# A sigmoid attention and token-mixing kernel: a new order of steps, loads and banks, merged stores, and the output weights rearranged by four transfers

## The chip, the cores and the metric

The kernel runs on one core of one Trainium2 chip. The metric is the device time of one execution in microseconds (us), the median over several runs. Lower is better.

## The reference

Attention with a sigmoid in place of the softmax, and on its output a layer that mixes tokens with weights made from the tokens themselves:

```python
# q, k, v: [8 batches, 12 heads, 448 tokens, 64]
scores = q @ k.T / sqrt(64) - log(448)
attn = 1 / (1 + exp(-scores))
x = (attn @ v)                      # heads side by side: [8, 448, 768]
wq, wk = x @ w_q, x @ w_k           # [8, 448, 64] each
W_tok = einsum('bsd,btd->bst', wq, wk) / sqrt(64)
mixed = einsum('bst,btd->bsd', W_tok, x)
out = maximum(mixed, 0) @ w_out     # [8, 448, 768], float32
```

## The kernel before

**Units of work.** Four heads of a batch make a quad; there are 24 quads (8 batches by 3). Tokens are numbered so that token = 7 p + i, with p on 64 partitions and i from 0 to 6, so each quad has 7 blocks of keys. One step `S` is one block: four score matmuls (L319) into two banks and one sigmoid of 128 x 896 elements on ScalarE, called ACT here (L324), into one of 16 `at` buffers. There are 168 such steps. A step `P` multiplies one block of `at` with the values (L341); after the seventh block of a quad the sum is copied out of the banks to `xt` (L348 in halves on two engines, L350 whole).

**What q, k and v go through.** The sync engine's queue (SP) loads each quad's q, k and v in float32 (L173, L179) into 8 buffers, GpSimd (POOL) or another engine casts them to bf16 (L192, L209, L215). Quads differ in how q and k are transposed. Kind `c` (14 quads): six copies of 32-partition pieces rearrange q and k on GpSimd (`arrange`, L161, L164, L167), then VectorE (DVE) transposes each whole (L276). Kind `r` (6 quads): VectorE transposes them in six pieces (L245, L269). Kinds `a` and `q`: TensorE (PE) transposes them (L237, L229), and VectorE copies the result.

**The mixing.** For each batch `tr_x` transposes `xt` to `xn` (L363, L379), `mlp_wqk` (L404, L416) makes wq and wk, `mlp_wkn` and `mlp_tmp` (L445, L460) and `mlp_mix` (L484, L498) follow, with the relu at L469 (ACT) or L471 (VectorE). The output product works on pairs of batches: `out_chunk` (L611) takes 128 tokens at a time for the first and the last pair, two token blocks of 64 at once, and stores them by `store` (L618 to L624), one transfer for each block; `out_pair` (L530) does the two pairs in the middle and `out_halves` (L570) a part of the last. `out_pair` and `out_halves` use a second copy of the output weights with its partition halves exchanged, made by step `C`, which moves `wout16` within the on-chip memory by SP (L864).

**The order.** Everything runs in an order written out by hand or by a planner: `PLAN` is a string with one letter for each step (`S`, `P`, `x` ...; a lower or an upper case often chooses the engine that copies a result out), `BANKS` says which of the eight PSUM banks each step takes, and `ORDER` is the order of the loads and casts; a dot there means a cast on VectorE, issued where `PLAN` has a `1`. Each engine executes its own instructions in that order and waits on semaphores. `pump_loads` issues a load as soon as the cast of the load eight before it has been issued; once `LATE` loads are out, only two more for each finished output chunk.

Of the kernel before, what the change touches and what calls it, by code (L numbers as in the profile page):

```python
# [17 lines left out]
def kernel(  # L18
# [12 lines left out]
    nc = tc.nc  # L31
    B, H, S, HD = q.shape
    D = H * HD
    DH = moe_w_q.shape[1]
    assert DH == HD == 64 and S == 448 and D == 768
    P = 128
    NI, NP = 7, 64
    NU = B
    NJ = H // 4
    NC = D // P  # L40
    NB = D // 2
    HALF = (slice(0, 64), slice(64, 128))
# [5 lines left out]
    def pool(name, bufs, **kw):  # L48
# [16 lines left out]
    banks16 = banks.rearrange("p b x -> p (b x)").bitcast(BF16).rearrange("p (b x) -> p b x", b=8)  # L65

    BANKS = (
# [11 lines left out]
    )  # L79
    BANKS = BANKS.split()[::-1]  # L80

# [25 lines left out]
    wout16 = singles.tile([P, 2 * NC, D], BF16, name="wout16")  # L107
# [17 lines left out]
    def xt(u, j):  # L125
        return xts[u % 2 * NJ + j]


    TW = (1, 2,)


    PLAN = (
        "FFSSSFFKSSF11aSSbFFrSFSFSSFSqSPPsPPSPzkPSPSPPPSxSrSsPPPPSPPS"
        "PSPPPPSSXWzSSwWWSWWXSNSSPPPrSsPPUSPPzSPSPSPCMPPPSPSqkSSMSXSM"
        "SCcPPPSPPxSPdPSOSwwrSSwwWWxSOSSOsOSNPPSPPzCPSPPSIISISIcPSPdP"
        "PSPS2SPPOOSxSUSPPSMPPPcSPPSdOwWwSSMWWWoSMPPSPPPP1SSPcdOQSxSO"
        "OSSNCSOOXcdSSOOSTSPPPSrPPCPSPPCPPSPPPSPSOwowSSSwsOzOxSwwWPSP"
        "MSPPPPRSScSdXXOXoSMSOoNSMPPSPcPPSPPSUdSOSMOSOMoPSPPcPPSPSdPw"
        "WXWSMSWWWXSSONOScTSOSOSOOdSPOSrOSPPPGPPSPPPSPPsPSPOSPOSOzSQS"
        "XPcPPSPPPSPOSOdSOSxOlLlSLlLPSPPPxPP2GSPOOScOmdOSOOSNO1SQSTPP"  # L140
        "PcS1PPSPOPSOSOQSMOSOSOdScOOSdOMSOmOP2PSPPxSPPP12SOSOSOSxOllL"
        "SllcSLPPPSPPPSPOOdSxSOOSOSOSONQSTPSPPPSPPPSPPPxPPmPPLxLlMlGL"
        "lOOyOoNIItIiIMimIiMOoOOOoOoOOOOOOOOOoOO"
    )
    KIND = ["a"] + [t for t in PLAN if t in "qacer"]

    ld = {}
    SRC = dict(q=q, k=k, v=v)
# [1 line left out]
    pq, arranged = {}, set()  # L150

    def arrange(n, eng):

        arranged.add(n)
        if KIND[n] in "er":
            return
        w = pq[n].rearrange("p e t i d y -> p e (t i d y)").bitcast(U32)
        z = p_one.tile([P, 2 * NI * 32], U32, tag="swap", name="swap")
        for g in range(2):
            lo, hi = slice(64 * g, 64 * g + 32), slice(64 * g + 32, 64 * g + 64)  # L160
            eng.tensor_copy(out=z[lo], in_=w[hi, 0])  # L161
        for g in range(2):
            lo, hi = slice(64 * g, 64 * g + 32), slice(64 * g + 32, 64 * g + 64)
            eng.tensor_copy(out=w[hi, 0], in_=w[lo, 1])  # L164
        for g in range(2):
            lo = slice(64 * g, 64 * g + 32)
            eng.tensor_copy(out=w[lo, 1], in_=z[lo])  # L167

    def load1(n, nm, eng):
        u, j = quads[n]  # L170
        if KIND[n] in "cer" and nm != "v":
            t = p_ld.tile([P, 2 * NI * HD], F32, tag="ld", name=nm + "32")
            eng.dma_start(  # L173
                out=t, in_=SRC[nm][u, 4 * j : 4 * j + 4].rearrange("h (p r) d -> (h p) (r d)", r=2 * NI),
            )
            ld[nm, n] = t
            return
        t = p_ld.tile([P, 2, NI * HD], F32, tag="ld", name=nm + "32")
        eng.dma_start(  # L179
            out=t,  # L180
            in_=SRC[nm][u, 4 * j : 4 * j + 4].rearrange(
                "(g h) (p i) d -> (h p) g (i d)", g=2, i=NI
            ),
        )
        ld[nm, n] = t

    def cast1(n, nm, e):
        if KIND[n] in "cer" and nm != "v":
            if n not in pq:
                pq[n] = p_c16.tile([P, 2, 2, NI, 32, 2], BF16, tag="qk16", name="qk16")  # L190
            f = pq[n]
            COPY[e](  # L192
                out=f[:, :, "qk".index(nm)].rearrange("p e i d y -> p e y i d"),
                in_=ld.pop((nm, n)).rearrange("p (y i e d) -> p e y i d", y=2, i=NI, e=2),
            )
            ld[nm + "16", n] = f
            if ("q16", n) in ld and ("k16", n) in ld:
                arrange(n, nc.gpsimd)
            return
        if nm == "v":  # L200
            t16 = p_v16.tile([P, 2, NI, HD], BF16, tag="v16", name="v16")
            if e == "d":
                u, j = quads[n]
                nc.gpsimd.dma_start(
                    out=t16.rearrange("p b i d -> p b (i d)"),
                    in_=v[u, 4 * j : 4 * j + 4].rearrange("(g h) (p i) d -> (h p) g (i d)", g=2, i=NI),
                )
            else:
                COPY[e](  # L209
                    out=t16.rearrange("p b i d -> p (b i d)"), in_=ld.pop((nm, n)).rearrange("p b x -> p (b x)"),  # L210
                )
            ld["v16", n] = t16
            return
        t16 = p_c16.tile([P, NI, 2, HD], BF16, tag=nm + "16", name=nm + "16")
        COPY[e](  # L215
            out=t16.rearrange("p i b d -> p b i d"),
            in_=ld.pop((nm, n)).rearrange("p b (i d) -> p b i d", i=NI),
        )
        ld[nm + "16", n] = t16
# [41 lines left out]
    def tr(n, nm, kind):  # L261
        t = "qk".index(nm)
        if kind == "s":
            return
        if kind == "r":
            qk[n] = p_qk.tile([P, 2, 2, NI, NP], BF16, tag="qk", name="qk")
            w = pq[n].rearrange("p e t i d y -> p e (t i d y)").bitcast(F32)
            for e in range(2):
                nc.vector.transpose(out=qk[n][:, e].rearrange("p t i n -> p (t i n)").bitcast(F32), in_=w[:, e])  # L269
            return  # L270
        if kind in "cdef":
            assert n in arranged
            w = pq[n].rearrange("p e t i d y -> p e (t i d y)").bitcast(F32)[:, t]
            if t == 0:
                qk[n] = p_qk.tile([P, 2, 2, NI, NP], BF16, tag="qk", name="qk")
            nc.vector.transpose(out=qk[n][:, t].rearrange("p t i n -> p (t i n)").bitcast(F32), in_=w)  # L276
            if kind in "ef":
                if t == 0:
                    moves.append((n, p_mv.tile([P, 2, 2 * S], BF16, tag="mv", name="mv")))
                nc.vector.transpose(out=moves[-1][1][:, t].bitcast(F32), in_=w)  # L280
            return
# [232 lines left out]
    def slot(half, b):  # L514

        return b // 2 + (0 if b % 2 == half else NC)

    def out_pair(act, split):

        if opened:  # L520
            w, blocks, part, fb, ps = opened.pop()
# [71 lines left out]
    def out_chunk(act, tail):  # L593
# [22 lines left out]
        last = w == NU // 2 - 1 and m == NI - 1  # L616

        def store(cols, eng=nc.scalar if tail else nc.sync):  # L618
            for y in range(2):
                b, i = divmod(2 * m + y, NI)  # L620
                (eng if y else nc.sync).dma_start(
                    out=out[2 * w + b].rearrange("(p i) d -> p i d", i=NI)[:, i, cols],
                    in_=o[HALF[y], cols],
                )  # L624
# [67 lines left out]
    for t in wqks:  # L692
# [1 line left out]


    ORDER = (
# [4 lines left out]
    )  # L701
    BY = {"s": [], "v": []}
    for x in ORDER.split():
# [7 lines left out]
    done = dict.fromkeys("SPqkKxWNUMOCgz", 0)  # L711
    used, loaded, cast = set(), set(), set()

    LATE = 44
    ring = [("q", 0), ("k", 0)]

    allowed = [2]
# [94 lines left out]
    used |= {("q", 0), ("k", 0)}  # L812
    pump()

    ALIKE = dict(a="q", c="q", e="q", r="q", b="k", d="k", f="k", s="k", j="k", h="k", X="x", y="x", Y="x", g="g", z="z", L="W", l="W", T="U", t="U", I="O", i="O", Q="O", G="M", R="P")
    done["q"] = done["k"] = 1
    quads_r = []

    for t in PLAN:
# [18 lines left out]
        elif kind in "qk":  # L838
# [4 lines left out]
            tr(c, kind, t)  # L843
            if t in "df":
                used.add(("q", c))
            if t not in "cers":
                used.add((kind, c))
                pump()
        elif t == "g":
# [10 lines left out]
        elif kind == "W":  # L860
            mlp_wqk(*divmod(c, NC), tail, t in "wl", t in "Ll")
        elif kind == "C":
            for y in range(2):
                nc.sync.dma_start(out=wout16[HALF[y], NC + c, :], in_=wout16[HALF[1 - y], c, :])  # L864
        elif kind == "N":
            mlp_wkn(c)
        elif kind == "U":
# [51 lines left out]
```

## Time and profile before

| what | value |
|---|---|
| median of 3 runs | 182.45 us (180.83 to 184.24) |
| span of the profiled execution (the page gives no other time for it) | 180.4 us |
| granted TensorE clock | 1.00 |
| busy: PE, DVE, ACT, POOL | 170.3, 143.7, 159.0, 122.9 us |
| sigmoids (L324) | 168, mean 951 ns each, 139.8 us in all |
| moved by DMA | 47.29 MB, 262 GB/s over the span |

The span runs from the first to the last instruction. Busy time is the union of an engine's instructions: two that overlap count once, so 168 sigmoids of 951 ns make 139.8 us. PE's matmuls are pipelined, and a PE that is busy all the time isn't at its peak for it. In lines by group, the columns are line, engine, operation, what is written and read with shapes and types, the number of instructions; then busy us and mean ns of one; then the idle time ahead of them, with what ended it.

### The profile page before, as it was taken

The page shows a single profiled execution, that of the slowest core. Times are in us where ns is not written, and L with a number is a line of the kernel's source. Part 1 is how long each engine was busy: PE and PEld are TensorE (multiplying, and loading weights), DVE is VectorE, ACT ScalarE, POOL GpSimd, SP SyncE. Part 2 cuts the span into 40 slices and gives each one's busy share as a digit, 9 for nine tenths or more (in the row PEclk, how much of TensorE's full clock was granted, in tenths as well). Part 3 has the DMA queues.
Part 4 walks back from the last instruction along what each step waited for, and adds up shares of the span by engine and source line. Part 5 has one row for each costly group of instructions (what it writes and reads, how often), then busy time and mean ns, then how long its engine had stood idle before and what let it go on. Part 6 is the DMA issues. An engine that isn't in the chain of part 4 may idle for free.

```text
span 180.4 us, 7849 instructions
## 1 busy us (share of the span) xinstructions
PE 170.3 (94%) x3412; PEld 114.1 (63%) x3412; DVE 143.7 (80%) x226; ACT 159.0 (88%) x208; POOL 122.9 (68%) x167
## 2 busy tenths in 40 slices
PE   7898899889999999999999999999999999999990
PEld 7444445444675555546667786677888888888660
DVE  3566899998988896989999999978789885868351
ACT  4599999999999999999999999998999989976310
POOL 1076899798999999999999999889978810010000
PEclk9999999999999999999999999999999999999999
DMA  5999999999999989699997999968596432505876
GB/s 169 353 394 346 325 385 376 283 304 366 339 305 358 349 266 299 226 318 349 279 318 277 257 307 329 372 215 272 137 336 166 131 88 48 137 4 123 207 196 174
DMA packets 24914, 47.29 MB, mean 262 GB/s; under 512 B 3888, under 2 KB 18480, under 8 KB 24880
## 3 DMA queue, kind: packets, MB, share of 16 engines
q1 hardware_dynamic: 23600, 44.64, 76.8%
q0 software_dynamic: 800, 1.18, 3.6%
q10 hardware_dynamic: 480, 0.98, 1.5%
q8 instruction: 26, 0.43, 0.9%
q14 instruction: 8, 0.07, 0.1%
HBM read 35.78 MB, written 11.01 MB: 259 GB/s over the span
## 4 chain that ended last, share of the span: by engine, by line
PE 61%; DMA 16%; ACT 7%; POOL 5%; DVE 4%; SPq 3%; issue 2%; POOLq 0%
PE banks L530 15%; PE banks L341 11%; PE banks L319 11%; PE banks L611 9%; DMA k<-in_k_dram 8%; ACT at L324 7%; DMA v<-in_v_dram 5%; DMA w<-in_moe_w_k_dram 4%; PE banks L570 3%; POOL qk L192 2%; PE banks L404 2%; PE banks L416 2%; PE banks L379 2%; PE banks L363 2%; PE banks L484 1%
## 5 line engine op out<-in xcount | busy, mean ns | idle before, releaser
L324 ACT ACTIVATE at<-banks 128x896 bf16<-128x896 f32 x168 | 139.8, 951 | 2.9 <-PE banks L319 2.4
L319 PE MATMUL banks<-qk 64*64 64x448 bf16 x672 | 62.0, 357 | 3.3 <-ACT at L324 2.0
L341 PE MATMUL banks<-at,v 64*64 64x448 bf16 x672 | 47.3, 351 | 0.8 <-ACT at L324 0.7
L319 PEld LDWEIGHTS <-qk 64*64 64x64 bf16 x672 | 25.7, 105 | 21.5 <-issue 13.3
L530 PE MATMUL banks<-wout,mx 64*64 64x384 bf16 x672 | 36.2, 323 | 0.0
L192 POOL CAST qk<-k 128x896 bf16<-128x896 f32 x19 | 22.7, 1196 | 10.1 <-DMA k<-in_k_dram 9.7
L341 PEld LDWEIGHTS <-v 64*64 64x64 bf16 x672 | 23.2, 106 | 8.4 <-issue 1.8
L350 DVE CAST xt<-banks 128x896 bf16<-128x896 f32 x22 | 23.8, 1084 | 2.5 <-PE banks L341 2.0
L530 PEld LDWEIGHTS <-mx 64*64 64x64 bf16 x672 | 22.6, 107 | 4.5 <-issue 0.2
L611 PE MATMUL banks<-wout,mx 128*128 128x384 bf16 (+1 forms) x138 | 24.4, 320 | 0.0
L192 POOL CAST qk<-q 128x896 bf16<-128x896 f32 x18 | 21.5, 1193 | 2.5 <-DVE qk L276 1.0
L471 DVE TENSOR_SCALAR mx<-banks 128x1024 bf16<-128x1024 f32 (+3 forms) x22 | 21.3, 970 | 1.9 <-PE banks L484 0.7
L209 POOL CAST v<-v 128x896 bf16<-128x896 f32 x22 | 20.6, 952 | 1.8 <-DMA v<-in_v_dram 1.3
L611 PEld LDWEIGHTS <-mx 128*128 128x128 bf16 x138 | 12.3, 98 | 9.8 <-issue 3.2
L167 POOL COPY qk<-swap 32x448 uint32<-32x448 uint32 x28 | 16.3, 584 | 1.6
L276 DVE STREAM_TRANSPOSE qk<-qk 128x448 f32<-128x448 f32 x28 | 17.0, 628 | 0.5 <-POOL qk L164 0.4
L161 POOL COPY swap<-qk 32x448 uint32<-32x448 uint32 x28 | 15.6, 556 | 2.5 <-DVE qk L192 0.8
L164 POOL COPY qk<-qk 32x448 uint32<-32x448 uint32 x28 | 15.6, 555 | 1.6
L245 DVE STREAM_TRANSPOSE qk<-qk 32x448 f32<-32x448 f32 x24 | 15.3, 636 | 0.6
L413 POOL COPY wq<-wqk 64x448 bf16<-64x448 bf16 x3 | 1.7, 556 | 15.8 <-DVE wqk L412 15.8
L644 DVE COPY o<-banks 128x384 f32<-128x384 f32 x12 | 6.6, 553 | 5.7 <-PE banks L611 5.3
L392 DVE COPY xn<-banks 128x1024 bf16<-128x1024 bf16 (+1 forms) x14 | 8.8, 625 | 2.8 <-PE banks L379 2.7
(89 smaller groups left out, 203.8 us busy)
## 6 DMA issues: line engine op xcount, KB each, us to landing
q<-in_q_dram SPq DMA_DIRECT2D x24, 448.0 KB, 6.3
v<-in_v_dram SPq DMA_DIRECT2D x24, 448.0 KB, 6.0
k<-in_k_dram SPq DMA_DIRECT2D x23, 448.0 KB, 6.9
out_dram<-o SPq DMA_DIRECT2D x50, 192.0 KB, 4.2
wout<-in_moe_w_out_dram POOLq DMA_DIRECT2D x2, 576.0 KB, 11.6
wout<-wout SPq DMA_DIRECT2D x12, 96.0 KB, 6.4
out_dram<-o ACTq DMA_DIRECT2D x4, 192.0 KB, 3.2
k<-in_k_dram SPq DMA_DIRECT2D x1, 256.0 KB, 4.8
```

The source lines that it names most:

```text
L161: eng.tensor_copy(out=z[lo], in_=w[hi, 0])
L167: eng.tensor_copy(out=w[lo, 1], in_=z[lo])
L192: COPY[e](out=f[:, :, "qk".index(nm)].rearrange("p e i d y -> p e y i d"), in_=ld.pop((nm, n)).rearrange("p (y i e d) -> p e y i d", y=2, ...
L209: COPY[e](out=t16.rearrange("p b i d -> p (b i d)"), in_=ld.pop((nm, n)).rearrange("p b x -> p (b x)"),)
L276: nc.vector.transpose(out=qk[n][:, t].rearrange("p t i n -> p (t i n)").bitcast(F32), in_=w)
L319: nc.tensor.matmul(sc[HALF[h], g, 0:S], qk[n][HALF[g], h, 1, i, :], qk[n][HALF[g], h, 0].rearrange("p i n -> p (i n)"), start=True, stop=True,
L324: inst = nc.scalar.activation(at, sc[:, :, 0:S], ACTF.Sigmoid, bias=attn_bias, scale=attn_scale)
L341: nc.tensor.matmul(ps[HALF[g], h, 0:S], ld["v16", n][HALF[h], g, i, :], ats[n, i][HALF[h], g, :], start=(i == 0), stop=(i == NI - 1),)
L350: read(fb, COPY[eng](out=xt(u, j)[:, :, 0:S], in_=ps[:, :, 0:S]))
L471: inst = nc.vector.tensor_scalar(dst, ps, moe_scale, 0.0, ALU.mult, ALU.max)
L530: nc.tensor.matmul(ps[HALF[x], y, 0:NB], mx[HALF[y], u, b, 64 * (i - 3 * y) : 64 * (i - 3 * y) + 64], wout16[HALF[y], slot(y, b), x * NB : ...
L611: nc.tensor.matmul(ps, mxs[w][:, 2 * S * c + m * P : 2 * S * c + (m + 1) * P], wout16[:, c, w0:w1], start=(c == 0), stop=(c == NC - 1),)
```

## The change

The three strings `PLAN`, `BANKS` and `ORDER` are replaced, and `LATE` goes from 44 to 58. In the new plan there are 15 quads of kind `c`, three of kind `r`, three of kind `q` and one of a new kind `v`, whose six rearranging copies run on VectorE. 14 casts stand on VectorE instead of six, none on ACT. More of the value sums and relus are copied out in halves, by VectorE and ACT (`R`, `G`). 24 of the 48 steps of `mlp_wqk` take its tiled form (L404) instead of 18.

The output weights' second copy is made by four transfers of 288 KB instead of twelve of 96 KB. The first two stand at the 26th and the 46th sigmoid, the other two at the 84th and the 86th.

`store` writes the two token blocks of a chunk by one transfer instead of two, unless the chunk belongs to the tail; the destination is an access pattern written out by hand. This concerns the seven chunks of the first pair of batches.

```diff
     PLAN = (
-        "FFSSSFFKSSF11aSSbFFrSFSFSSFSqSPPsPPSPzkPSPSPPPSxSrSsPPPPSPPS"
...
+        "FFSSSFFKSSFS1abSpRSPS1PSPPSrszSSPPSP1pPSRSPSPSqSXSkSPRRRpSRr"
...
-    KIND = ["a"] + [t for t in PLAN if t in "qacer"]
+    KIND = ["a"] + [t for t in PLAN if t in "qacerv"]
...
             if ("q16", n) in ld and ("k16", n) in ld:
-                arrange(n, nc.gpsimd)
+                if KIND[n] == "v":
+                    arranged.add(n)
+                else:
+                    arrange(n, nc.gpsimd)
...
+        if kind == "v":
+            arrange(n, nc.vector)
-        if kind in "cdef":
+        if kind in "cdefv":
...
+    def rows(b0, i0, b1, i1):
+
+        step = (b1 - b0) * S * D + (i1 - i0) * D
+        assert step > 0
+        return out[b0].rearrange("(p i) d -> p i d", i=NI)[:, i0], [step, 2]
...
         def store(cols, eng=nc.scalar if tail else nc.sync):
+            if not tail and cols == slice(0, D):
+                (b0, i0), (b1, i1) = divmod(2 * m, NI), divmod(2 * m + 1, NI)
+                at, lead = rows(2 * w + b0, i0, 2 * w + b1, i1)
+                nc.sync.dma_start(out=bass.AP(at.tensor, at.offset, [lead, [NI * D, NP], [1, D]]), in_=o)
+                return
             for y in range(2):
...
-    LATE = 44
+    LATE = 58
...
         elif kind == "C":
-            for y in range(2):
-                nc.sync.dma_start(out=wout16[HALF[y], NC + c, :], in_=wout16[HALF[1 - y], c, :])
+            if c % 3 < 2:
+                y, lo = c % 3, c // 3 * 3
+                nc.sync.dma_start(
+                    out=wout16[HALF[y], NC + lo : NC + lo + 3, :], in_=wout16[HALF[1 - y], lo : lo + 3, :],
+                )
```

More of the change, by code (lines that the diff above doesn't have):

```diff
@@ L126, in xt @@
         return xts[u % 2 * NJ + j]
-    TW = (1, 2,)
+    TW = (1, 2, )
     PLAN = (
-        "FFSSSFFKSSF11aSSbFFrSFSFSSFSqSPPsPPSPzkPSPSPPPSxSrSsPPPPSPPS"
[L134 to L143, printed above, removed]
+        "FFSSSFFKSSFS1abSpRSPS1PSPPSrszSSPPSP1pPSRSPSPSqSXSkSPRRRpSRr"
+        "SPXSSSsWCWWzWSWWSXPSPNSSvdpUSSpSRPPSSMSXMSqSkSPPPPSMRSRSPPPP"
+        "SpRRSPScWCWWodSxSWOWSSWOSSOoOSNxSOcSdSOOQSpSRRPrPRsSPRPzRSPp"
+        "PRSSUXSpRpGG1PPSpP1SWooSMSWCXWSqkSXWWSScSWQdOQcSSNSd1OoOS1TS"
+        "PpSRRpPRMScPPSRpPRSSPOXSOdSRpCSxpPPSCRPSo1WSOSMSWWOScMSOWWWS"
+        "SdSOORNR1SRPxPSRPcSQSOdSCTSpRPSPPpSPOSOSMOSORPcSRSpxRPRLLSLS"
+        "1LLLQSodSQNGQSxoScQMSOSdOSPRPRSppPSQ1SQxcSoSOSUSRdRpGPpSPPSP"
+        "PRpGRSR1PSoQScQSOSdLLLLSLLRSPRRPGpSPQSoxSQcQSxoSOdSx1QSOpSpR"
+        "PSRNpPSQScOSxodSOSTQSOSOGOSO1SOGOcSpOSPRGdpPRSPxQOSOoSLxLLcL"
+        "LSLSdRPpPpSPROOSNOSOSpppPSRRRSTSOoSOSORSPRPpGLRpLLLmyLLoyyQo"
+        "NMQtIIiMiiMiiGioooOQQoQOoOQOOOoOQoQ"
     )
-    KIND = ["a"] + [t for t in PLAN if t in "qacer"]
+    KIND = ["a"] + [t for t in PLAN if t in "qacerv"]
     ld = {}
@@ L154, in arrange @@
         arranged.add(n)
-        if KIND[n] in "er":
+        if KIND[n] in "r":
             return
@@ L170, in load1 @@
         u, j = quads[n]
-        if KIND[n] in "cer" and nm != "v":
+        if KIND[n] in "crv" and nm != "v":
             t = p_ld.tile([P, 2 * NI * HD], F32, tag="ld", name=nm + "32")
@@ L187, in cast1 @@
     def cast1(n, nm, e):
-        if KIND[n] in "cer" and nm != "v":
+        if KIND[n] in "crv" and nm != "v":
             if n not in pq:
@@ L813 @@
     pump()
-    ALIKE = dict(a="q", c="q", e="q", r="q", b="k", d="k", f="k", s="k", j="k", h="k", X="x", y="x", Y="x", g="g", z="z", L="W", l="W", T="U", t="U", I="O", i="O", Q="O", G="M", R="P")
+    ALIKE = dict(v="q", a="q", c="q", e="q", r="q", b="k", d="k", f="k", s="k", j="k", h="k", X="x", y="x", Y="x", g="g", z="z", L="W", l="W", T="U", t="U", I="O", i="O", Q="O", G="M", R="P")
     done["q"] = done["k"] = 1
@@ L845 @@
                 used.add(("q", c))
-            if t not in "cers":
+            if t not in "cersv":
                 used.add((kind, c))
```

30 rows, old and new, of tables (BANKS, ORDER) are left out of this document.

## The prediction

> **What bounds the kernel now.** I read the page's busy shares first, then ACT's groups, then four stretches of the span, and the transfers last.
>
> ```profile
> span 180.4 us, 7849 instructions
> PE 170.3 (94%) x3412; PEld 114.1 (63%) x3412; DVE 143.7 (80%) x226; ACT 159.0 (88%) x208; POOL 122.9 (68%) x167
> L324 ACT ACTIVATE at<-banks 128x896 bf16<-128x896 f32 x168 | 139.8, 951 | 2.9 <-PE banks L319 2.4
> 39.30 11.60 ACT L324 ACTIVATE at<-banks 128x896 bf16<-128x896 f32 x14
> ```
>
> The last row is from the timeline of ACT: 14 sigmoids back to back in 11.60 us, 0.83 us each. All 168 have 139.8 us of busy time, and ACT idled only 2.9 us ahead of them in the whole kernel. So ACT sets the pace from the first to the last sigmoid, and a sigmoid is a good clock: I call the place between two sigmoids in the plan a beat. The next view gives ACT's L324 alone in four stretches, and under it all engines in the same ones (busy us with counts for PE, PEld, DVE, ACT, POOL, then clock, DMA share, GB/s).
>
> ```profile
> 0.00:46.00 46.00, 39.03 (x49) 1.00 1.01 332
> 46.00:100.00 54.00, 50.49 (x61) 1.00 0.93 302
> 100.00:157.00 57.00, 50.28 (x60) 1.00 0.72 220
> 157.00:180.40 23.40, 0.00 (x0) 1.00 0.53 137
> ...
> 0.00:46.00 46.00, 40.91 (x712) 22.65 (x712) 35.95 (x64) 41.51 (x53) 31.71 (x42) 1.00 1.01 332
> 46.00:100.00 54.00, 53.86 (x926) 32.69 (x925) 48.15 (x72) 52.90 (x68) 50.73 (x70) 1.00 0.93 302
> 100.00:157.00 57.00, 56.37 (x1438) 44.69 (x1440) 47.56 (x69) 55.26 (x71) 39.87 (x56) 1.00 0.72 220
> 157.00:180.40 23.40, 19.16 (x344) 14.09 (x336) 12.00 (x24) 9.29 (x20) 0.56 (x1) 1.00 0.53 137
> ```
>
> From 46 to 100 us, 61 beats take 54 us, 0.885 us each (54 / 61); after that 0.95 (57 / 60). ACT and PE are both full there, POOL is at 94%, and the transfers at 93%: nothing has room to spare but the lead with which loads arrive. After 157 us no sigmoid is left and PE's output products make a tail of 23.4 us.
>
> **The edits that nearly cancel.** I counted each engine's operations in both plans from the code. The rows that carry the differences:
>
> ```profile
> L469 ACT ACTIVATE mx<-banks 128x512 bf16<-128x512 f32 (+1 forms) x4 | 3.2, 808 | 0.5 <-PE banks L484 0.5
> L644 ACT COPY o<-banks 128x384 f32<-128x384 f32 x5 | 2.5, 498 | 0.2 <-ACT at L324 0.2
> L541 ACT COPY o<-banks 128x384 f32<-128x384 f32 x4 | 1.9, 481 | 0.0
> L209 ACT CAST v<-v 128x896 bf16<-128x896 f32 x1 | 0.9, 930 | 0.0
> L348 ACT CAST xt<-banks 128x448 bf16<-128x448 f32 x1 | 0.5, 538 | 0.0
> ...
> L469 ACT ACTIVATE mx<-banks 128x512 bf16<-128x512 f32 x2 | 1.2, 600 | 0.5 <-PE banks L484 0.5
> ...
> L209 POOL CAST v<-v 128x896 bf16<-128x896 f32 x22 | 20.6, 952 | 1.8 <-DMA v<-in_v_dram 1.3
> L864 SPq DMA_DIRECT2D wout<-wout x12: 467/522/897, 41.7 to 87.8; - x12
> ...
> L611 PE MATMUL banks<-wout,mx 128*128 128x384 bf16 (+1 forms) x138 | 24.4, 320 | 0.0
> L570 PE MATMUL banks<-wout,mx 64*64 64x384 bf16 x144 | 7.3, 324 | 0.0
> L821 PE MATMUL banks<-zeros 128*128 128x512 bf16 x10 | 3.8, 432 | 0.0
> ...
> L209 DVE CAST v<-v 128x896 bf16<-128x896 f32 x1 | 1.1, 1060 | 0.0
> L245 DVE STREAM_TRANSPOSE qk<-qk 32x448 f32<-32x448 f32 x24 | 15.3, 636 | 0.6
> L276 DVE STREAM_TRANSPOSE qk<-qk 128x448 f32<-128x448 f32 x28 | 17.0, 628 | 0.5 <-POOL qk L164 0.4
> ```
>
> ACT, ahead of the last sigmoid: nine relus on halves (9 x 0.60 = 5.4) for four (3.2), four L348 more (2.2), three L644 fewer (1.5), two L541 (1.0) and one v cast (0.9) fewer: 2.2 + 2.2 - 1.5 - 1.0 - 0.9 = +1.0 us, on the path. Back to back a sigmoid costs 0.83 us though it lasts 0.951, so neighbours overlap by some 0.12, and three operations more may cost as little as +0.6. I take +1. PE: 12 more L611 (24.4 x 12 / 138 = 2.1) for 48 fewer L570 (7.3 / 3 = 2.4), five fillers fewer at the start; the tail after the last sigmoid has the same list but four L341 matmuls fewer. Zero. VectorE: 12 fewer L245 (7.6 us) against five more v casts (5.3), four more L276 (2.5) and the six copies of 32 partitions that kind v moves from GpSimd to it (no row shows them on VectorE; between nothing and L245's 0.636 each, 3.8 together; I take 2). About +2 us on an engine with 5.9 us spare from 46 to 100 us; covered, and 2 us if that cover goes. GpSimd has three casts L192 (1.2 us, below) and four L209 (0.95) fewer and six copies of 32 partitions (0.58, below) more: 4 us less, off the path. The output weights' move becomes four issues instead of twelve with the same bytes: it saves SP 8 x 0.52 = 4 us of issue, and ACT's idle time is ended by PE, not by transfers, so nothing on the path. Its first piece now stands at beat 26 behind the weights' own load, and the loads q9 to k11 wait behind it on SP; they are wanted from beat 57 on, and cover is ample. The new load order and LATE = 58 change when SP issues the same loads, not their bytes; with the DMA share at 1.01 up to 46 us and ACT's 39.03 us of sigmoids there, I take zero, a us either way. The best that the new order can do is to take the 2.9 us of ACT's idle time. Together with the +1 that is a gain of 1.9 us at most.
>
> **The edit that doesn't cancel: the merged store.** Seven stores (the chunks of the first pair of batches, at beats 52, 56, 65, 75, 83, 92 and 99) were two transfers each, of 64 rows of 3 KB. Now each is one, and its destination is written by hand as [2 blocks][64 rows][768], the count of 2 outermost. How is a transfer shared among the 16 DMA engines?
>
> ```profile
> q10 hardware_dynamic: 480, 0.98, 1.5%
> ...
> q10 hardware_dynamic: 80, 0.20, 10.0%
> ...
> q1 hardware_dynamic: 5960, 13.70, 91.7%
> ```
>
> The first row is ACT's own queue, which carries six stores only (L621): 480 packets are 6 x 64 rows and 6 x 16 closing packets, one from each engine. The second is that queue from 168 to 173 us, a single store: 80 packets = 64 + 16, taking 10.0% of 16 engines x 5 us = 8.0 engine-us. Spread over 16 it costs each 0.5 us. The third is SP's queue from 50 to 95 us. Every transfer of the kernel before has 64 or 128 outermost, so no row shows what a count of 2 does. The bounds are: still sixteen (1.0 us an engine for both blocks, nothing changed) or two engines, each with one block of 64 rows: 8.0 us on each of two engines. I take the second: 64 row packets and 16 closings mean that rows, the outermost step, were dealt whole, four to an engine; nothing seen here cuts an outermost step, and this pattern has only two of them to deal.
>
> [...]
>
> What it does: I take it that transfers of one queue go through each engine in order (a load lands 6.3 us after its issue, by a row below, though its work is 1.17 us an engine: it stands behind others). So the loads that SP issues behind a store wait on those two engines, and a load is complete only when all its 16 parts are. A load of 448 KB is worth 448 / 192 x 8.0 / 16 = 1.17 us on each engine. I write the queue of the two slow engines out, with a beat b at 46 + 0.885 (b - 49) us up to 100 us and 0.95 after:
>
> - five loads issued at beat 46 (43.3 us) end at 49.2; store 1 (beat 52) at 57.2; store 2 (beat 56) at 65.2
> - four loads (beats 63, 64) 69.9; store 3 (beat 65) 77.9; three loads 81.4; store 4 (beat 75) 89.4
> - seven loads 97.6; store 5 (beat 83) 105.6; the weights' move 107.1; q17, k18, q18 110.6
> - store 6 (beat 92) 118.6; v16, v17 120.9; store 7 (beat 99) 128.9; v19, q19 131.2
> - two ordinary stores 132.2; k19 133.4
>
> Then the way from a load to its transposes, from GpSimd's timeline:
>
> ```profile
> 92.25 1.21 POOL L192 CAST qk<-k 128x896 bf16<-128x896 f32 x1
> 93.52 1.17 POOL L161 COPY swap<-qk 32x448 uint32<-32x448 uint32 x2
> 94.75 1.17 POOL L164 COPY qk<-qk 32x448 uint32<-32x448 uint32 x2
> 95.98 1.17 POOL L167 COPY qk<-swap 32x448 uint32<-32x448 uint32 x2
> ```
>
> From cast to the last copy 4.9 us, and I estimate 1.5 us from the last packet to the load's semaphore, since the quickest stores of the row below land 2.5 us after their issue with little to move. q15 and k15 are wanted at beat 99 (90.3 us) and are there at 97; k19 is wanted at beat 131 (119.9 us) and is there at 133.4 + 1.5 + 4.9 = 139.8: 20 us late. ACT waits for PE, PE for VectorE's transposes, those for GpSimd, GpSimd for the load. After store 7 the plan has no slack with which to catch up. Late next: all that follows, the tail included.
>
> ```profile
> out_dram<-o SPq DMA_DIRECT2D x2, 96.0 KB, 2.5
> out_dram<-o SPq DMA_DIRECT2D x50, 192.0 KB, 4.2
> q<-in_q_dram SPq DMA_DIRECT2D x24, 448.0 KB, 6.3
> GB/s 297 318 282 273 358 366 351 349 404 358 277 332 255 192 341 237 360 338 244 72 289 320 233 307 347 414 381 325 310 403 340 151 161 372 375 299 279 363 284 66
> ...
> q1 hardware_dynamic: 23600, 44.64, 76.8%
> ```
>
> Bounds of the price: the busiest slice of 48 to 100 us moved 414 GB/s, 25.9 an engine, so 196,608 bytes take 7.6 us; over the whole run an engine made 44.64 MB / (0.768 x 16 x 180.4 us) = 20.1 GB/s, 9.8 us. Seven stores at 7.6, and the loads in proportion, make it 15.5 us late; at 9.8, with some 26 loads at 1.43, it is 39. I stay with 8.0, the duration of such a store itself, because two engines that run on alone have the memory to themselves.
>
> **Sum.** The page gives the profiled execution no time but its span, 180.4 us: 180.4 + 20 = 200.4, where the +1 on ACT is lost in ACT's new idle time. The runs shown have a median of 182.45, 2 us above that span; I put the same 2 us on top: **202 us**. Its own range is 195 to 219 (15.5 and 39 late, less the 2.9 us that the new order may save at the low end).
>
> **The rivals.**
>
> 1. *The merged store is still shared by all sixteen engines* (chance 0.22). For it: 80 packets and 16 closings in every transfer seen; against it: none seen has so few outer steps. Then the stores cost what they did, and the place that decides is ACT's 2.9 us idle ahead of L324: with all of it gained and the +1 paid, 182.45 - 1.9 = 180.5; with none gained, 183.5. It would have to gain over 3.65 us to be faster by 2%, more than ACT's idle time, so that needs the stretched pitch after 100 us (0.95 a beat against 0.885, up to 3.9 us) to shrink too: then 177. Of the 0.22 I give 0.09 to that and 0.13 to no change.
> 2. *Two engines, but the lead hides it* (0.05). For it: up to eight loads can be out, worth 8 x 7 / 3 = 18.7 beats, 16.5 us. Against it: from 50 to 95 us the engines were busy at 91.7% already, so 45 us have some 4 us free, and seven stores ask 7 x 7.0 = 49 us more. If lead and free time hide all but a little: 183 to 187.
> 3. *VectorE becomes the bound* (0.05). By count, beats 72 to 84 now hold 18 of its operations, 12.4 us at their rows' durations, where 12 beats last 10.6. Price 2 us there and as much in beats 144 to 156; stores shared by sixteen: 182.45 + 4 = 186.5.
>
> **How the numbers follow.** My forecast has 0.68. A measurement of this kernel can tell about 2% from no change (its three runs lie 1% to either side). Slower by over 2%: 0.68, plus 0.03 of rival 2, plus rival 3's 0.05: 0.76. Within 2%: 0.13 and 0.02: 0.15. Faster: 0.09. The range of 8 in 10 goes from 180, which takes in most of rival 1, to 216, leaving out the gain and the highest price.
>
> **What would show it.** Right: the seven stores of 384 KB take over 9 us from issue to landing (the median of the 50 of half that size was 4.2); GpSimd's casts at L192 and L209 wait for DMA by 15 us or more in total, between 85 and 140 us, and ACT idles about as long ahead of L324; the mean DMA share from 46 to 110 us falls well below 0.93, since fourteen engines wait for two; the first 49 sigmoids and the tail of 23 us stay as they are. Wrong: stores that land in 5 us, or ACT's idle time still under 5 us. Then the count of 2 is not what shares out a transfer, and only the order is left to explain the time.

## The result, and the profile after

| kernel | median us (lowest to highest) | profiled span |
|---|---|---|
| before | 181.64 (180.78 to 184.24) | 180.4 |
| changed | 216.87 (214.61 to 218.08) | 214.5 |

The ratio is 1.1875 (95% interval 1.1741 to 1.2009). The forecast was 202 us and slower; the measured median lies 0.9 us above the stated range of 180 to 216 and within the forecast's own range of 195 to 219. In some executions a kernel here takes 1 to 2% longer than in the others (in the first experiment 192.2 and 193.0 us beside 188.7 and 189.5): medians are of all executions, ratios of the others alone, and microseconds called "by the ratio" are worked out from ratios with 182 us for the kernel before. The page after, with a row of the page before for the packets:

```profile
span 214.5 us, 7978 instructions
PE 178.0 (83%) x3493; PEld 117.1 (55%) x3493; DVE 147.3 (69%) x230; ACT 162.7 (76%) x213; POOL 122.3 (57%) x166
L329 ACT ACTIVATE at<-banks 128x896 bf16<-128x896 f32 x168 | 142.1, 937 | 30.9 <-PE banks L324 30.3
```

The engines' busy times are those of before within 8 us; what is new is ACT's idle time ahead of the sigmoids, 30.9 us where it was 2.9. L324 of the kernel before is L329 now, L319 is L324, and the merged store is L633. ACT's L329 alone, and under it all engines, in stretches:

```profile
0.00:46.00 46.00, 34.83 (x43) 0.96 0.99 321
46.00:100.00 54.00, 45.76 (x54) 0.97 0.66 227
100.00:157.00 57.00, 33.38 (x40) 0.85 0.63 198
157.00:190.00 33.00, 28.09 (x33) 1.00 0.56 163
190.00:214.50 24.50, 0.00 (x0) 0.95 0.57 147
...
46.00:100.00 54.00, 50.30 (x821) 28.31 (x816) 41.66 (x65) 47.81 (x60) 32.00 (x43) 0.97 0.66 227
100.00:157.00 57.00, 40.41 (x872) 28.42 (x868) 32.83 (x46) 35.83 (x46) 40.68 (x56) 0.85 0.63 198
```

Six sigmoids were lost before 46 us already (43 for 49), seven from 46 to 100, twenty from 100 to 157. After that the pace is the old one (33 in 33 us), and the tail of 24.5 us is about the old one. From 46 to 157 us the DMA share is 0.66 and 0.63, where it was 0.93 and 0.72. How the transfers stood, from 60 to 66 us, when the first merged stores ran:

```profile
DMA  2212101111111111111111111111161111115925
GB/s 77 77 65 82 75 20 61 41 41 41 61 41 61 41 61 41 61 61 41 61 41 61 41 61 41 61 41 61 61 150 61 41 61 41 61 61 89 232 85 157
q1 hardware_dynamic: 123, 0.37, 19.5%
```

The digits are tenths of sixteen engines in forty slices. A row of ones and 41 to 61 GB/s for five microseconds is two engines of sixteen, at some 25 GB/s each, while fourteen have nothing to move. The number of engines can also be counted. Packets of the kernel before, and after:

```profile
DMA packets 24914, 47.29 MB, mean 262 GB/s; under 512 B 3888, under 2 KB 18480, under 8 KB 24880
DMA packets 24193, 47.31 MB, mean 221 GB/s; under 512 B 3550, under 2 KB 17630, under 8 KB 24158
```

There are 338 fewer packets under 512 B. SP issues 15 transfers fewer (seven for stores, eight for the weights), which takes away 15 x 16 = 240 closings; the other 98 are 7 x 14, so each of the seven merged stores leaves 2 closings and not 16. Who waited, on GpSimd from 50 to 190 us, and then pieces of the chain that ended last (start us, us, what):

```profile
POOL v L212 <- DMA v<-in_v_dram: 12.2, 2, 7.7
POOL qk L192 <- DMA k<-in_k_dram: 6.0, 3, 4.5
POOL qk L192 <- DMA q<-in_q_dram: 4.9, 2, 4.6
...
66.30 12.89 DMA v<-in_v_dram
...
80.95 18.79 DMA k<-in_k_dram
...
119.02 18.76 DMA out_dram<-o
```

GpSimd waits 23.1 us for loads; before, in the same part of the kernel, it waited for none. A load of 448 KB that took 6.3 us at the median takes up to 18.8 behind the stores. The last of the seven 384 KB stores stands on the chain; it landed at 119.02 + 18.76 = 137.8 us.

SP itself was held as well. Its issue of the load behind the first two stores, and of one kind of load in all (ns, shortest, median and longest; the kernel before, then the changed one):

```profile
57.78 7.12 SPq L173 DMA_DIRECT2D q<-in_q_dram  x1
...
L173 SPq DMA_DIRECT2D q<-in_q_dram x20: 327/344/1803, 3.8 to 121.6; - x20
L173 SPq DMA_DIRECT2D q<-in_q_dram x19: 340/632/7117, 3.8 to 165.5; - x19
```

Until 64.9 us SP was on this one load, and it issued the next at 65.4, so the fourteen engines also had no further load to start on. What holds an issue for so long no run here shows.

### The profile page after: what moved, and what is told of

Read it like the earlier page. It is cut to its first block, busy times and chain, and to the rows that moved or that the text cites. A ratio compares the mean times of both kernels' runs of the same rounds, so it can differ in the third digit from the quotient of the medians.

```text
span 214.5 us, 7978 instructions
## 1 busy us (share of the span) xinstructions
PE 178.0 (83%) x3493; PEld 117.1 (55%) x3493; DVE 147.3 (69%) x230; ACT 162.7 (76%) x213; POOL 122.3 (57%) x166
## 4 chain that ended last, share of the span: by engine, by line
PE 43%; DMA 34%; DVE 14%; SPq 3%; POOL 2%; ACT 2%; issue 1%; DVEq 0%
DMA k<-in_k_dram 12%; PE banks L541 12%; DMA out_dram<-o 9%; PE banks L324 8%; PE banks L622 7%; DMA wout<-wout 7%; PE banks L346 6%; DMA v<-in_v_dram 6%; DVE qk L248 3%; DVE xt L355 2%; PE banks L581 2%; PE banks L409 2%; ACT at L329 2%; PE banks L384 2%; SPq L881 2%; POOL qk L192 1%
## 5 line engine op out<-in xcount | busy, mean ns | idle before, releaser
L329 ACT ACTIVATE at<-banks 128x896 bf16<-128x896 f32 x168 | 142.1, 937 | 30.9 <-PE banks L324 30.3
L324 PE MATMUL banks<-qk 64*64 64x448 bf16 x672 | 66.5, 370 | 11.4 <-DVE tmp L454 4.2
L324 PEld LDWEIGHTS <-qk 64*64 64x64 bf16 x672 | 28.0, 108 | 31.2 <-issue 19.7
L541 PE MATMUL banks<-wout,mx 64*64 64x384 bf16 x672 | 39.6, 336 | 6.3 <-DVE o L554 5.8
L622 PE MATMUL banks<-wout,mx 128*128 128x384 bf16 (+1 forms) x150 | 27.7, 328 | 8.4 <-DVE xn L397 7.7
L346 PEld LDWEIGHTS <-v 64*64 64x64 bf16 x672 | 25.6, 109 | 9.9 <-issue 2.6
L212 POOL CAST v<-v 128x896 bf16<-128x896 f32 x18 | 17.6, 984 | 15.2 <-DMA v<-in_v_dram 14.9
L476 DVE TENSOR_SCALAR mx<-banks 128x448 bf16<-128x448 f32 (+3 forms) x24 | 20.1, 840 | 3.0 <-PE banks L489 1.5
L355 DVE CAST xt<-banks 128x896 bf16<-128x896 f32 x18 | 19.5, 1083 | 3.6 <-PE banks L346 3.3
L281 DVE STREAM_TRANSPOSE qk<-qk 128x448 f32<-128x448 f32 x32 | 19.9, 630 | 0.7 <-POOL qk L164 0.7
L161 POOL COPY swap<-qk 32x448 uint32<-32x448 uint32 x30 | 18.2, 608 | 2.2 <-DVE qk L167 0.4
L554 DVE COPY o<-banks 128x768 f32<-128x768 f32 x10 | 9.5, 946 | 10.7 <-DMA out_dram<-o 6.3
```

The source lines that it names most:

```text
L212: COPY[e](out=t16.rearrange("p b i d -> p (b i d)"), in_=ld.pop((nm, n)).rearrange("p b x -> p (b x)"),)
L324: nc.tensor.matmul(sc[HALF[h], g, 0:S], qk[n][HALF[g], h, 1, i, :], qk[n][HALF[g], h, 0].rearrange("p i n -> p (i n)"), start=True, stop=True,
L329: inst = nc.scalar.activation(at, sc[:, :, 0:S], ACTF.Sigmoid, bias=attn_bias, scale=attn_scale)
L346: nc.tensor.matmul(ps[HALF[g], h, 0:S], ld["v16", n][HALF[h], g, i, :], ats[n, i][HALF[h], g, :], start=(i == 0), stop=(i == NI - 1),)
L355: read(fb, COPY[eng](out=xt(u, j)[:, :, 0:S], in_=ps[:, :, 0:S]))
L476: inst = nc.vector.tensor_scalar(dst, ps, moe_scale, 0.0, ALU.mult, ALU.max)
```

## The experiments

**Two stores again.** Only the branch in `store` is taken out:

```diff
-            if not tail and cols == slice(0, D):
...
-                nc.sync.dma_start(out=bass.AP(at.tensor, at.offset, [lead, [NI * D, NP], [1, D]]), in_=o)
-                return
```

> The changed kernel with each of the seven merged stores written as two transfers of 64 rows again, all else as changed. Theory A (a merged store runs on two DMA engines and the loads behind it wait): the delay from 55 us on goes away and only the 5 us that the changed kernel had lost before its first merged store stay: 185 us, 182 to 190; GpSimd waits for DMA by under 8 us after 50 us. Rival B (the new order of steps and loads is what starves ACT): 210 us or more.

Measured 190.87 us (188.73 to 192.97), 1.0451 of before (1.0332 to 1.0571). So 26 us of the 34 hang on the merged store by the ratio (1.1875 - 1.0451), and rival B falls. The median lies 0.9 us over the expected range, with its four times on both sides of the bound. By the ratio 8.2 us are left to something else, where 5 were expected. Transfers from 60 to 66 us in this kernel, and GpSimd's longest waits from 50 to 166 us:

```profile
DMA  9879999999999899999998999989899996799975
q1 hardware_dynamic: 922, 2.18, 98.0%
...
POOL wq L418 <- DVE wqk L417: 6.9, 2, 5.5
POOL qk L192 <- issue: 5.0, 2, 3.7
```

All engines are busy, 2.18 MB against 0.37 in the same six microseconds, and no wait of GpSimd's is for a transfer. SP's longest issue of a load took 1.8 us.

**The merged store alone, in the kernel before.** The same branch added to its `store`; six chunks take it there, not seven, since one chunk of that pair goes by `out_halves`.

> The kernel before with its six whole-chunk stores of the first pair merged by the same hand-written destination, nothing else changed. Theory A: the queue of two slow engines written out for the old order of loads makes k19 some 20 us late, and the changed kernel was later than that sum gave: 200 to 215 us, small packets 6 x 30 = 180 fewer (six transfers and 6 x 14 closings fewer). Rival B: 180 to 183 us, the merged store saves only issue time.

Measured 206.07 us (204.97 to 207.79), ratio 1.1397 (1.128 to 1.1513), 25 us over before by the ratio. Nothing else of the change is in it. Its page has 3708 packets under 512 B, 180 fewer than before, as expected for two closings each, SP's longest issue of a load took 6.9 us, and the wait is the same one:

```profile
POOL qk L192 <- DMA k<-in_k_dram: 19.7, 5, 8.6
ACT at L324 <- PE banks L319: 16.6, 17, 7.1
```

**Half of the bytes.** The left half of the columns goes by a merged transfer, the right half by two ordinary ones:

```diff
-                nc.sync.dma_start(out=bass.AP(at.tensor, at.offset, [lead, [NI * D, NP], [1, D]]), in_=o)
-                return
+                nc.sync.dma_start(
+                    out=bass.AP(at.tensor, at.offset, [lead, [NI * D, NP], [1, NB]]), in_=o[:, 0:NB],
+                )
+                cols = slice(NB, D)
```

> The changed kernel with the left 384 columns of a chunk's two blocks in one merged transfer and the right 384 in two of 64 rows, so that half of the bytes go by the pattern with 2 outermost. Theory A: 4.0 us on the two engines for each chunk and 0.5 for the rest; by the queue written out k19 is there at 115.6 us, 4 us ahead of its need, so nearly all of the delay goes: 185 to 192 us. Rival C (each merged transfer costs a fixed time whatever its bytes, for instance because its semaphore blocks SP's queue): 210 us or more, since seven merged transfers remain.

Measured 195.41 us (194.53 to 196.31), ratio 1.0804 (1.0694 to 1.0913): 6.4 us over the run with two stores by the ratio, where all of the bytes cost 26, and 3.4 us over the expected range. A fixed cost for each merged transfer (rival C) falls: seven are still there. Half of the bytes leaves a quarter of the delay, which is what a queue with some lead would do; that by the queue written out nearly all of it would go was too favourable. GpSimd waits 7.6 us for loads after 50 us instead of 23.1, and SP's longest issue of a load is 1.8 us again.

**The rearranging copies on GpSimd.** Besides two stores, the letter `v` in `PLAN` becomes `c`.

> As the changed kernel with two transfers for each store, and besides the quad of kind v made kind c, so that its six rearranging copies run on GpSimd and not on VectorE. Theory A with the loss before the first store put down to these copies (6.4 us of VectorE between 30.1 and 36.5 us, ahead of a 3.6 us gap on ACT): 3 to 4 us less than with two stores alone, 179 to 184 us. Rival: the gap comes from the order of the loads, and the time stays within 1 us of that run.

Measured 185.87 us (184.44 to 187.97), ratio 1.0245 (1.0118 to 1.0373), and 185.92 when it was run again (ratio 1.0255, 1.0187 to 1.0323, an interval that ends below that of two stores alone). The edit is worth 3.7 us by the ratio, as expected. The time itself is 1.9 us over the expected range, since the run with two stores came out above its own. In the changed kernel, VectorE's copies from 29 to 38 us and the gap behind them on ACT:

```profile
L167 DVE COPY qk<-swap 32x448 uint32<-32x448 uint32 x2 | 2.2, 1124 | 0.1
L164 DVE COPY qk<-qk 32x448 uint32<-32x448 uint32 x2 | 2.0, 1004 | 0.1
L161 DVE COPY swap<-qk 32x448 uint32<-32x448 uint32 x2 | 2.0, 980 | 0.1
...
38.84 1.92 ACT L329 ACTIVATE at<-banks 128x896 bf16<-128x896 f32 x2 [3.64 <-PE banks L324]
```

**Kind v in the kernel before.** Quad 7 becomes kind `v`, with the code that the change adds for it; the order stays.

> The kernel before with quad 7 made kind v: its six rearranging copies stand on VectorE at the place of its transposes (beat 46, wanted at beat 49) and not on GpSimd. If VectorE copies 32 partitions in 1.0 us each, as in the changed kernel, 6.2 us stand ahead of the transposes with 3 beats (2.5 us) of lead: 3 to 5 us slower, 185.5 to 188. If the copies cost what the forecast took (0.34 us each, 2 us together): within 0.5 us of before.

Measured 187.08 us (185.22 to 187.62), 1.0199 of before (1.0149 to 1.0249), 3.6 us over before by the ratio. The time is as expected, but its reason is not. The `v` stands at beat 42, not 46, and the copies took this long (timelines of VectorE and of GpSimd):

```profile
40.00 0.80 DVE L161 COPY swap<-qk 32x448 uint32<-32x448 uint32 x2
40.83 1.68 DVE L164 COPY qk<-qk 32x448 uint32<-32x448 uint32 x2
42.54 0.80 DVE L167 COPY qk<-swap 32x448 uint32<-32x448 uint32 x2
...
40.83 1.43 POOL L192 CAST qk<-q 128x896 bf16<-128x896 f32 x1 [1.30 <-DVE swap L161]
43.12 1.26 POOL L192 CAST qk<-k 128x896 bf16<-128x896 f32 x1 [0.85 <-DMA k<-in_k_dram]
...
43.94 0.65 DVE L397 COPY xn<-banks 128x1024 bf16<-128x1024 bf16 x1
...
L622 PE MATMUL banks<-wout,mx 128*128 128x384 bf16 (+1 forms) x138 | 24.3, 320 | 2.9 <-DVE xn L397 2.9
L329 ACT ACTIVATE at<-banks 128x896 bf16<-128x896 f32 x168 | 140.1, 951 | 6.3 <-PE banks L324 5.7
```

0.4 us each while GpSimd is idle, 0.84 beside its cast, which itself takes 1.43 instead of 1.2. So the six take 3.3 us and not 6.2. What they delay is not the transposes but a copy of `xn` in VectorE's order behind them: it starts at 43.94 us, before at 41.41. PE waits 2.9 us for it ahead of an output product, where it waited for nothing (L611 before), and ACT's idle time goes from 2.9 to 6.3 us, nearly all of the 3.6.

**Four moves of the output weights, both ways.** In the kernel before, the step `C` as changed; in the changed kernel with two stores and kind `c`, the step `C` as before.

> The kernel before with the output weights moved by four transfers of 288 KB (beats 35, 42, 77 and 83), nothing else changed. Off the path, as forecast: within 1 us of before. If the larger moves hold up the loads behind them or the first one waits for the weights longer: 1 to 3 us slower. If the saved issue time counts: 1 to 3 us faster.

Measured 184.22 us (182.14 to 185.77), ratio 1.0043 (1.0002 to 1.0084): off the path, as forecast.

> The changed kernel with two transfers for each store and kind c for v, and the output weights moved by twelve transfers of 96 KB at the new places. If four moves save what SP's issue time says (8 x 0.52 us) on the path, this is 2 to 4 us slower: 188 to 190. If they are off the path, as forecast: 184.5 to 187.5.

Measured 192.44 us (191.26 to 194.12), ratio 1.0502 (1.045 to 1.0554), well over both expectations; that is 4.5 us by the ratio over the same kernel with four moves. One wait is as long as that, and it isn't issue time. In the new plan the last of the six steps `C` stands at the 100th sigmoid, where the four-move form does nothing; with twelve moves the last piece starts only there, and PE waits for it:

```profile
PE banks L541 <- DMA wout<-wout: 4.6, 1, 4.6
```

**LATE.** In the kernel before set to 58; in the changed kernel with two stores and kind `c` set back to 44.

> The kernel before with LATE 58. In the old order the loads from the 45th on are held to two for each output chunk; with 58 they go out earlier, ahead of stores. ACT idles 2.9 us in all before its last sigmoid and the loads after 100 us land well before their casts: within 1 us of before. If loads that go out earlier stand in the way of nearer ones: 1 to 3 us slower.

Measured 183.25 us, ratio 1.0055 (1.0015 to 1.0095): 1 us by the ratio, off the path as forecast.

> The changed kernel with two transfers for each store and kind c for v, and LATE back at 44. If the remaining 3 us over the kernel before come from loads let out too freely ahead of the stores: 183 us. If they come from the order of the steps (theory A has nothing else left): within 1.5 us of the same kernel with LATE 58, 184.5 to 187.5.

Measured 191.08 us, ratio 1.0332 (1.0281 to 1.0383), over both expectations and about 1% over the same kernel with 58 by the ratios, with intervals that overlap (1.0187 to 1.0323 for the repeat). If anything the new order wants 58; the value isn't where its remaining loss comes from.

**Four v casts back on GpSimd.**

> The changed kernel with two transfers for each store and kind c for v, and the casts of v15, v16, v20 and v21 on GpSimd (0.95 us each) and not on VectorE (1.06 us each). If the new order's remaining loss is VectorE's load: 1 to 3 us less than the same kernel with those casts on VectorE, run beside it. If VectorE has room there, as the forecast took it: within 1 us of it, or slower where a v cast now stands behind others in GpSimd's queue.

Measured 187.57 us (186.2 to 190.15; ratio 1.0316, 1.0249 to 1.0384) beside 185.92 (1.0255) for the same kernel with them on VectorE. It isn't faster, so the load of these casts on VectorE isn't the remaining loss. No version here beats the kernel before.

## Why the prediction was right, and where its sizes were off

*What bounds the kernel*: right. ACT set the pace, and what made it wait came through nearly in full: it idled 28 us more ahead of the sigmoids, and the last sigmoid ended 33 us later.

*The merged store*: right, two engines; no row of before had a count of 2, so that was an estimate from 64 + 16 packets, and the page after shows 2 closings for each merged store. The wait went the way described, from the load to GpSimd's cast, the transposes, the scores and ACT. The term was 20 us and measured 26 in the new order and 25 in the old. The queue written out let store 7 end at 128.9 us; it landed at 137.8. Most of that was there at the first store: the prediction's beats put it at 48.7 us, and it was issued at 55.2. The six copies aren't the reason, since without them it went out at 55.5. From the first issue to the last landing 82.6 us passed, where the prediction has 80.2, so the price of 8.0 us for a store wasn't too low. That this length came out so near is in part luck, since the prediction has no term for the issues that held SP for up to 8.0 us. What else is in the 6 us between 20 and 26 no run separates.

*Kind v*: the term that failed. The prediction gave the six copies 2 us on VectorE, covered by 5.9 us of spare time. They took 6.2 us at one place, ahead of the transposes of a quad that was due five beats later, and cost 3.7 us by the ratio. The spare time was a mean from 46 to 100 us, and the copies stand at 30 us, where the kernel before leaves VectorE (third of the busy times) next to none:

```profile
30.00:40.00 10.00, 8.77 (x188) 4.70 (x184) 9.78 (x13) 10.00 (x13) 8.64 (x13) 1.00 1.10 301
```

Cover is what stands between one instruction and its due time. The upper bound taken from L245 (0.64 us each) was also too low.

*The order*: +1 on ACT with a gain of up to 2.9 was forecast. What stays with two stores and kind `c` is 2.5% (1.0255), 4.6 us by the ratio and 3.5 us in the profiled spans (183.9 and 180.4). ACT there:

```profile
L329 ACT ACTIVATE at<-banks 128x896 bf16<-128x896 f32 x168 | 140.8, 939 | 5.3 <-PE banks L324 4.4
L474 ACT ACTIVATE mx<-banks 128x512 bf16<-128x512 f32 (+1 forms) x9 | 5.4, 625 | 0.0
```

With 26 for the stores and 3.7 for the copies these 4.6 make up the 34 us. The relus cost the 5.4 us of the sum, but ACT's idle time went up to 5.3 us instead of down, in nine gaps of under 0.9 us each. Why PE is late for it, and why the tail is a microsecond longer, stays open. LATE at 44, twelve moves and four v casts put back each made this kernel no faster, so none of them explains it alone; their places in the new order were not varied.

*Moves of the weights and LATE*: zero, right in the old order; in the new one the form of the moves matters, since with twelve the last would come too late. The prediction didn't look at that, as it saw them as off the path.

*Rivals*: sixteen engines: no, two closings each. The lead hides it: no, and for half of the bytes only in part. VectorE as the bound: not by its load, but for six copies in a row, yes.

*Signs named in advance*: the 18.76 us of the last store, GpSimd's waits for loads (21.3 us of the 23.1 between 85 and 140 us) and the fall of the DMA share came true. That the first 49 sigmoids stay as they are did not, for the copies; the tail stayed within about a microsecond.

## What to carry to other kernels

Two transfers made into one can be slower by far, here by 26 us for seven stores: look at the outermost count of each access pattern (here the destination's was 2, with 128 partitions on the other side), and count the closing packets in the profile (2 for a merged store, 16 for each of the two it replaces), since the bytes and the number of issues don't tell. A transfer on few engines was paid for here by the loads queued behind it, and not in proportion to its bytes: half of them left a quarter of the delay (6.4 of 26 us). Cover for an added instruction is the slack of those behind it on its engine, of whatever kind, and not the engine's mean spare time (in the kernel before, 3.3 us of copies cost 3.6 us).

## What was not expected of the hardware

TensorE's granted clock, 1.00 in the profile before, fell to half in pieces of the changed one. From 100 to 112 us PE worked 4.3 us only, and the clock (the third number from the end) was 0.62 on the mean, 0.50 from 104 to 112 us:

```profile
100.00:112.00 12.00, 4.30 (x42) 1.57 (x38) 3.89 (x6) 2.75 (x4) 11.16 (x17) 0.62 0.63 193
132.00:142.00 10.00, 4.22 (x89) 2.97 (x85) 2.67 (x4) 3.15 (x4) 2.32 (x2) 0.76 0.75 234
```

While matmuls were still to come, the clock was at 0.50 in four pieces: from 38.1, 79.1, 103.0 and 137.1 us on, for 3 to 10 us each. PE's wait in or ahead of each was 4.2, 1.6, 7.7 and 5.8 us; in a wait of 2.7 us, up to 128.7 us, the clock stayed at 1.00. So the length of the wait alone doesn't decide it, and what does no run here shows. Each such piece then costs a little more: in these pieces the score matmuls took 548 to 577 ns each on the mean, from 46 to 75 us 360, and all 672 took 370, where they took 357 before. VectorE's copies between places of the on-chip memory took 0.4 us with GpSimd idle, 0.84 beside its cast (kind `v` in the kernel before) and 0.98 to 1.12 beside its casts in the changed kernel. Why they take longer there is open: no run here took the work beside them away by itself.
